# A recurrence feeding routed experts: the inverse grown in PSUM, decays exchanged on TensorE, loads multiplied in place, and a new start

## The chip, the cores and the metric

The kernel runs on one core of one Trainium2 chip. The metric is the device time of one execution in microseconds (us); the time given for a kernel is the median of its runs. The engines are TensorE (PE, with its weight loads as PEld), VectorE (DVE), ScalarE (ACT), GpSimd (POOL) and SyncE (SP, which here only issues DMAs). All numbers are 32-bit floats.

## The reference, cut to what matters

Four batches, eight heads, 768 steps, head size 40. For every step a 40 x 40 state is read by r, decayed by w, changed by a and b, and added to by v and k. The result, 3072 rows of 320, goes through one of eight expert networks (320 to 1024 to 320), chosen for each row by its token number.

```python
for t in range(S):
    y[:, :, t] = einsum('bhd,bhde->bhe', rt, state)
    Sa = einsum('bhde,bhe->bhd', state, at)
    state = state * wt[:, :, None, :] - einsum('bhd,bhe->bhde', Sa, bt)
    state = state + einsum('bhd,bhe->bhde', vt, kt)
x = y.transpose(0, 2, 1, 3).reshape(B * S, H * D)
expert_idx = token_ids * 2654435761 % E
out[expert_idx == e] = maximum(x[expert_idx == e] @ w1[e], 0) @ w2[e]
```

## The kernel before, in words

**Chunks and tiles.** Time is cut into 12 chunks of 64 steps. A tile is one chunk of two batches (two halves of 64 partitions) with all eight heads; there are 24 tiles, u = 0 to 23, and even and odd tiles carry the states of different batches. Inside a chunk, the 64 steps become matrix products: the products of decays up to each step (p) and from each step to the end (q) scale a, b and k, and the dependence of a step on those before it becomes a triangular matrix that has to be inverted, in blocks of 32.

**The plan.** Every step of the attention part is a small function put into a list with a time in ticks (`at_tick`). The list is sorted, and its functions are called in that order. PE, DVE, ACT and POOL carry out their instructions in just this order (`manual_schedule`, L780); SP's DMAs are not in that list before the change, and the framework orders them. Each engine works through its own queue in order and waits where an operand isn't there. One tick is about one tile's work on PE. Tile u is prepared around tick u and goes through the recurrence at tick u + 8 (LAG), so ticks 0 to 7 only prepare, 8 to 23 do both, 24 to 31 only the recurrence.

**Decays** (L216 to L325). Six rounds, each of two chunks, hence four tiles. w is loaded to 128 partitions (four sub-blocks of 32 batch-heads, 32 steps each). DVE clamps it and counts the clamped values into `wbad` (L249, L250), multiplies up p and q in segments of eight steps (L263, L268), and takes products of whole segments (`own`). The two halves of a chunk lie on different partitions, so they exchange their end products through DRAM: store, load, store (L279, L280, L287), and L315 loads the ends again to form `pend` with PE. Then POOL does two wide products (L296, L302) and stores p and q to DRAM as rows (L233), four DMAs each.

**Tile, first part** (`tile_a`). At u - 2, SP loads p, q (L347, L348), a, b, k (L193) to `pl`, `al`, `ql`, `kb`. At u - 1.3, POOL multiplies: `at` = a p (L360), `z` = (b, k) q (L362). PE turns both (t_ps L412, z_ps L379), ACT copies them back. At tick u PE forms a_ps; ACT copies part of it to `pk`, DVE masks the rest to `mk` (L403), POOL makes `no` (L401).

**Inverse** (`group_i`). For four tiles together, DVE builds the inverse of 32 x 32 blocks, one per partition and head, in `ub` in SBUF: POOL fills it with the identity (L428, L429), then 31 times DVE forms `outer` (L444) and adds it to `ub` (L447), spread over 3.4 ticks. Two DVE transposes give `ut` and `ug` (L455, L456). PE uses them in x_ps (at tick u + 7 plus a fraction) and u_ps; ACT and POOL make `xi` and `um`.

**Recurrence** (`tile_s`, `tile_b`). r and v are loaded (L193) and turned on PE one after the other (r_t, v_t). PE's steps are r_ps (r0, r1), c_ps, rc_ps (rc_v, rc_c), nc_ps, s_ps, y_ps, sd_ps. DVE masks rc_ps to `mr` (L581), scales s_ps by `pend` to `sc` (L600), scales y_ps by `py` to `xs` (L618); POOL loads `py` (L510) and stores xs (L621). Within a tick the order is that of STEPS (L200). PSUM is used in three buffers of two banks (`psa`) and two of one bank (`psb`).

**Experts** (L859 on). Once the attention is done, its buffers are given up, SP loads the weights (L86, L88, L799), POOL gathers rows (L805) and scatters results (L836), PE does up_ps and dn_ps. At the end the sum of `wbad` decides whether a slow path has to run. It doesn't with these inputs.

Of the kernel before, what the change touches and what calls it, by code (L numbers as in the profile page):

```python
# [8 lines left out]
F32 = mybir.dt.float32  # L9
# [9 lines left out]
def kernel(  # L19
# [61 lines left out]
    wbad = route.tile([P, 2 * S * B * H // (C * P)], F32)  # L81
# [18 lines left out]
    psa = apool("psa", 3, space=bass.MemoryType.PSUM)  # L100
    psb = apool("psb", 2, space=bass.MemoryType.PSUM)

# [25 lines left out]
    at_r, r1_r = (ring(n, 2, [P, HP, R], gap) for n in ("at", "r1"))  # L128
    r_r = ring("r", 2, [P, HP, P], gaps)
    x_r = ring("x", 3, [P, 2, HP, P], gaps2)  # L130
    z_r = ring("z", LAG + 2, [P, 2, HP, R], gap)


    st_r = ring("st", NG, [R, 2, HP, 2, D], all_of)
    sd_r = ring("sd", NG, [R, 2, HP, 2, D], all_of)
    sc_r = ring("sc", NG, [R, 2, HP, D], all_of)
    at_t_r = ring("at_t", LAG, [P, 2 * HP * C + BLK], lambda t: t[:, 2 * HP * C:])
    en_r = ring("en", 2, [BLK, HP, P], all_of)
# [4 lines left out]
    nc.vector.memset(first[:], 0.0)  # L143
    for be in range(2):
        rows = slice(be * C, (be + 1) * C)
        nc.vector.tensor_tensor(after[rows], upper[rows, rows], ones[rows, rows], op=OP.mult)
        nc.vector.memset(first[be * C:be * C + BLK], 1.0)
        rows = slice(be * C + BLK, (be + 1) * C)
        nc.vector.tensor_copy(xi_r(0)[rows, :, BLK:C], ident[rows, rows].unsqueeze(1).to_broadcast([BLK, H, BLK]))


# [3 lines left out]
    end_dram = [nc.dram_tensor(f"end{i}", (RN, 3, B * H, D), F32) for i in range(NR)]  # L155
# [34 lines left out]
    def load(dst, src, b0, t0, crossed=False):  # L190

        for be in range(2):
            nc.sync.dma_start(dst(be, half(1 - be if crossed else be)),  # L193
                              src[b0 + be, :, t0:t0 + C, :].rearrange("h t e -> t h e"))

    tiles = [dict() for _ in range(NU)]
    plan = []


    STEPS = ["c", "rc_v", "x", "sd", "nc", "rc_c", "u", "a", "r_t", "v_t", "s", "y", "r0", "r1", "at_t", "z"]  # L200

    def at_tick(tick, step=None, order=0):
        if step is not None:
            tick += STEPS.index(step) / len(STEPS)

        def add(f):
            plan.append((round(tick, 4), order, len(plan), f))
            return f
        return add
# [6 lines left out]
    def decays(ri, t0, span, t_ends):  # L216
# [8 lines left out]
        def segs(t):  # L225
            return t[:, 0:HC * D].rearrange("p (s t e) -> p s t e", s=SEG, e=D)


        BH = B * H

        def store(i, src):
            for y in range(2 * RN):
                nc.gpsimd.dma_start(pq_dram[ri][i][y * HC:(y + 1) * HC].rearrange("t bh e -> bh t e"),  # L233
                                    src[y * BH:(y + 1) * BH].rearrange("p (t e) -> p t e", e=D))

        def ends_rows(i):

            return end_dram[ri][:, i:i + 2].rearrange("n x bh e -> n (x bh) e")

        @step  # L240
        def _():
            x["pb"] = pb = work.tile([P, HC * D], F32, tag="pb", name="pb", bufs=1)
            x["qb"] = qb = work.tile([P, (HC + 1) * D], F32, tag="qb", name="qb", bufs=1)
            for y in range(2 * RN):
                src = w.rearrange("b h (n t) e -> (b h) n (t e)", t=HC)[:, ri * 2 * RN + y]
                nc.sync.dma_start(pb[y * BH:(y + 1) * BH], src)
            nc.sync.dma_start(end_dram[ri][:, 2], ones[0:RN * BH, 0:D])
            q = qb[:, 0:HC * D]
            nc.vector.tensor_scalar(q, pb[:], LO, HI, op0=OP.max, op1=OP.min)  # L249
            nc.vector.scalar_tensor_tensor(pb[:], q, 0.0, pb[:], op0=OP.add, op1=OP.not_equal,  # L250
                                           accum_out=wbad[:, ri:ri + 1])

        @step
        def _():
            nc.vector.memset(segs(x["pb"])[:, :, 0, :], 1.0)


        qs = [x_ for x_ in range(SL - 2, -1, -1)]
# [5 lines left out]
        for i in qs:  # L264
            @step
            def _(i=i):
                q = segs(x["qb"])
                nc.vector.tensor_tensor(q[:, :, i], q[:, :, i], q[:, :, i + 1], op=OP.mult)  # L268

        @step  # L270
        def _():

            q = segs(x["qb"])
            x["own"] = own = work.tile([P, SEG, D], F32, tag="own", name="own", bufs=1)
            x["ends"] = ends = work.tile([P, SEG + 1, D], F32, tag="ends", name="ends", bufs=1)
            nc.vector.tensor_copy(own[:, SEG - 1], q[:, SEG - 1, 0])
            for s in range(SEG - 2, -1, -1):
                nc.vector.tensor_tensor(own[:, s], q[:, s, 0], own[:, s + 1], op=OP.mult)
            nc.sync.dma_start(ends_rows(0), own[:, 0])  # L279
            nc.sync.dma_start(ends[:, SEG], ends_rows(1))  # L280

        @step
        def _():
            ends = x["ends"]
            nc.vector.tensor_tensor(ends[:, 0:SEG], x["own"][:],
                                    ends[:, SEG].unsqueeze(1).to_broadcast([P, SEG, D]), op=OP.mult)
            nc.sync.dma_start(ends_rows(0), ends[:, 0])  # L287
            x["rends"] = rends = work.tile([P, SEG, D], F32, tag="rends", name="rends", bufs=1)
            nc.vector.reciprocal(rends[:], ends[:, 0:SEG])
            nc.vector.tensor_scalar(rends[:], rends[:], -1.0, None, op0=OP.mult)  # L290

        @step
        def _():

            p = segs(x["pb"])
            nc.gpsimd.tensor_tensor(p, p, x["rends"][:].unsqueeze(2).to_broadcast([P, SEG, SL, D]), op=OP.mult)  # L296
            store(0, x["pb"][:])

        @step
        def _():  # L300
            q = segs(x["qb"])
            nc.gpsimd.tensor_tensor(q, q, x["ends"][:, 1:].unsqueeze(2).to_broadcast([P, SEG, SL, D]),  # L302
                                    op=OP.mult)
            nc.gpsimd.tensor_copy(x["qb"][:, HC * D:], x["ends"][:, SEG])
            store(1, x["qb"][:, D:])

        for i, f in enumerate(todo):
            at_tick(t0 + span * i / len(todo), order=8)(f)

        @at_tick(t_ends)  # L310
        def _():

            en = en_r(ri)
            for rn in range(RN):
                nc.sync.dma_start(en[rn * B:(rn + 1) * B].rearrange("b hp (two x) -> b (hp two) x", two=2)[:, :, 0:D],  # L315
                                  end_dram[ri][rn, 0].rearrange("(b h) e -> b h e", h=H))

        @at_tick(t_ends + 1.0)
        def _():
            en = en_r(ri)  # L320
            p = bank([P, HP, B * RN], "en_ps")
            for hp in range(HP):
                nc.tensor.transpose(p[0:R, hp, :], en[0:B * RN, hp, 0:R], ident[0:B * RN, 0:B * RN])
            x["pend"] = t = work.tile([P, HP, RN, B], F32, tag="pend", name="pend", bufs=NR)
            nc.scalar.copy(t[0:R].rearrange("p h n b -> p h (n b)"), p[0:R])  # L325
# [4 lines left out]
    def tile_a(u):  # L330
# [5 lines left out]
        @at_tick(u - 2.0)  # L336
        def _():
            x["p"] = pl = work.tile([P, DM], F32, tag="pl", name="pl")
            x["a"] = al = work.tile([P, DM], F32, tag="al", name="al")
            x["q"] = ql = work.tile([P, 2, DM], F32, tag="ql", name="ql")  # L340
            x["kb"] = kb = work.tile([P, 2, DM], F32, tag="kb", name="kb")

            def by_head(t):
                return t.rearrange("t (h e) -> t h e", h=H)
            p_rows, q_rows = (d[rn * C:(rn + 1) * C] for d in pq_dram[ri])
            for be in range(2):
                nc.sync.dma_start(pl[half(be)], of_batches(p_rows, 2 * g + be, 1))  # L347
                nc.sync.dma_start(ql[half(be)], of_batches(q_rows, 2 * g, 2))  # L348
            load(lambda be, rows: by_head(al[rows]), a, 2 * g, n * C)

            load(lambda be, rows: by_head(kb[rows, be]), b, 2 * g, n * C)
            load(lambda be, rows: by_head(kb[rows, be]), k, 2 * g, n * C, crossed=True)

        @at_tick(u - 1.3)
        def _():
            x["at"], x["z"] = at_r(u), z_r(u)

            def view(t):
                return t.rearrange("p (hp two e) -> p hp two e", hp=HP, two=2)
            nc.gpsimd.tensor_tensor(heads(x["at"]), view(x["a"][:]), view(x["p"][:]), op=OP.mult)  # L360
            for be in range(2):
                nc.gpsimd.tensor_tensor(heads(x["z"][:, be]), view(x["kb"][:, be]), view(x["q"][:, be]), op=OP.mult)  # L362
# [639 lines left out]
```

## Time and profile before

| What | us |
|---|---|
| median of the runs | 867.81 |
| lowest and highest of 3 runs | 861.88, 875.35 |
| profiled execution, its own time | 872.0 |
| its span, first to last instruction | 870.1 |
| PE busy in the span | 654.8 |
| DVE busy | 380.2 |
| POOL busy | 317.2 |
| ACT busy | 222.0 |

Busy times overlap, so they don't add up to the span. The page cuts the span into 40 slices of about 21.75 us and gives each engine's busy share in tenths. PE is nearly idle in the first seven, and near full from the tenth on, but for one in the middle where the attention ends and the experts begin. A row of a group reads: line, engine, operation, output and inputs by name, shapes, count. A row of waits reads: engine and line that waited, what released it, total us, times, longest. The clock column is the granted TensorE clock as a share of full speed.

### The profile page before, as it was taken

How to read it: one execution, taken by the hardware profiler on the slowest of the kernel's cores; microseconds unless marked ns; L12 is line 12 of the kernel's file. 1: busy time of each engine (PE TensorE's matmuls, PEld its weight loads, DVE VectorE, ACT ScalarE, POOL GpSimd, SP SyncE). 2: the span in 40 equal slices, each digit the busy share in tenths (PEclk: the TensorE clock that was granted, in tenths of full speed). 3: DMA queues.
4: the chain of work that ended last, by engine and by line, in shares of the span. 5: the costliest groups of instructions: out<-in, count | busy, mean ns of one | idle time of the engine just before them, and what ended most of it. 6: DMA issues, size and time to landing. Idle time of an engine off the chain costs nothing.

```text
span 870.1 us, 27167 instructions
## 1 busy us (share of the span) xinstructions
PE 654.8 (75%) x11952; PEld 501.2 (58%) x11952; DVE 380.2 (44%) x758; ACT 222.0 (26%) x464; POOL 317.2 (36%) x416
## 2 busy tenths in 40 slices
PE   0023532199769986989998999982999999999993
PEld 0012421188658875878787888871556656655652
DVE  7051659567865775666666567121111111011110
ACT  0011211034333442445433434430111111111010
POOL 4617481452274338645534513214022013011101
PEclk9999999998765876678767869996999999999997
DMA  3646484364456446545522223319733226221000
GB/s 70 127 109 137 105 183 96 64 139 86 80 98 140 90 82 120 96 89 110 97 47 41 48 38 60 65 26 303 265 104 100 81 63 200 79 76 36 23 3 25
DMA packets 166793, 82.66 MB, mean 95 GB/s; under 512 B 139982, under 2 KB 156111, under 8 KB 166672
## 3 DMA queue, kind: packets, MB, share of 16 engines
q1 hardware_dynamic: 157264, 56.94, 29.1%
q0 software_dynamic: 9408, 23.95, 11.7%
q8 instruction: 95, 1.56, 0.8%
q14 instruction: 26, 0.21, 0.1%
HBM read 64.78 MB, written 16.40 MB: 93 GB/s over the span
## 4 chain that ended last, share of the span: by engine, by line
PE 60%; DVE 16%; POOL 8%; DMA 7%; issue 4%; SPq 3%; ACT 1%; POOLq 0%; DVEq 0%; ACTq 0%
PE dn_ps L846 12%; PE up_ps L826 11%; PE s_ps L181 6%; PE y_ps L181 5%; PE r_ps L181 4%; DVE ub L447 4%; PE up_ps L822 3%; PE u_ps L181 3%; PE a_ps L181 3%; PE rc_ps L181 3%; PE t_ps L412 3%; DVE outer L444 2%; DMA end<-own 2%; DMA ends<-end 2%; DVE pb L263 2%
## 5 line engine op out<-in xcount | busy, mean ns | idle before, releaser
L846 PE MATMUL dn_ps<-w,ht 128*128 128x320 f32 x384 | 104.9, 433 | 0.0
L447 DVE TENSOR_TENSOR ub<-ub,outer 128x31 f32<-128x31 f32 (+15 forms) x186 | 98.6, 530 | 6.3
L836 POOL DMA_INDIRECT out_dram<-o,idx_all x26 | 25.9, 997 | 187.5 <-ACT o L835 182.6
L826 PE MATMUL up_ps<-xt,w 128*128 128x416 f32 x256 | 93.8, 519 | 0.0
L846 PEld LDWEIGHTS dn_ps<-w,ht 128*128 128x128 f32 x384 | 72.8, 190 | 32.1 <-issue 1.9
L621 POOL DMA_DIRECT2D x_rows<-xs x48 | 27.3, 570 | 159.4 <-DVE outer L444 80.4
L444 DVE TENSOR_TENSOR outer<-ub,nb 128x31 f32<-128x31 f32 (+15 forms) x186 | 72.7, 391 | 21.6 <-POOL ub L429 17.8
L412 PE MATMUL t_ps<-ident,at 64*104 64x64 f32 x192 | 13.0, 269 | 82.2 <-POOL at L360 82.2
L826 PEld LDWEIGHTS up_ps<-xt,w 128*128 128x128 f32 x256 | 47.5, 190 | 45.8 <-issue 45.8
L829 DVE TENSOR_SCALAR ht<-up_ps 128x416 f32<-128x416 f32 x32 | 18.9, 591 | 105.8 <-PE up_ps L826 101.4
L181 PE MATMUL a_ps<-at_t,z_t 40*32 40x64 f32 (+1 forms) x2304 | 52.3, 290 | 13.9 <-ACT z_t L380 7.2
L412 PEld LDWEIGHTS t_ps<-ident,at 64*104 64x104 f32 x192 | 8.9, 157 | 84.0 <-POOL at L360 82.5
L811 DVE COPY xt<-xg_ps 128x384 f32<-128x384 f32 x24 | 12.1, 551 | 102.1 <-PE xg_ps L810 102.1
L181 PEld LDWEIGHTS a_ps<-at_t,z_t 40*32 40x32 f32 (+1 forms) x2304 | 43.0, 157 | 20.8 <-issue 11.0
L181 PE MATMUL x_ps<-ut,no 32*32 32x32 f32 x768 | 19.6, 204 | 45.0 <-DVE ut L455 44.1
L181 PEld LDWEIGHTS s_ps<-x,z 128*64 128x64 f32 (+1 forms) x704 | 36.7, 187 | 19.7 <-issue 19.7
L362 POOL TENSOR_TENSOR z<-kb,ql 128x320 f32<-128x320 f32 x48 | 43.0, 917 | 10.0 <-DMA ql<-q_rows 5.4
L581 DVE TENSOR_TENSOR mr<-rc_ps,after 128x1024 f32<-128x1024 f32 x24 | 29.3, 1221 | 39.5 <-PE rc_ps L181 39.5
L181 PEld LDWEIGHTS x_ps<-ut,no 32*32 32x32 f32 x768 | 16.5, 118 | 47.3 <-DVE ut L455 32.0
L403 DVE TENSOR_TENSOR mk<-a_ps,after 128x512 f32<-128x512 f32 x24 | 16.5, 688 | 56.8 <-ACT pk L399 56.8
L181 PE MATMUL s_ps<-x,z 128*64 128x40 f32 (+1 forms) x704 | 40.0, 280 | 1.0 <-issue 1.0
L296 POOL TENSOR_TENSOR pb<-pb,rends 128x1280 f32<-128x1280 f32 x6 | 17.3, 2888 | 61.2 <-DVE rends L290 61.2
(164 smaller groups left out, 1262.7 us busy)
## 6 DMA issues: line engine op xcount, KB each, us to landing
w<-in_moe_w_dram SPq DMA_DIRECT2D x8, 1280.0 KB
w<-in_moe_w_dram SPq DMA_DIRECT2D x8, 1024.0 KB
ql<-q_rows SPq DMA_DIRECT2D x48, 160.0 KB
pb<-in_w_dram SPq DMA_DIRECT2D x24, 160.0 KB
al<-in_a_dram SPq DMA_DIRECT2D x48, 80.0 KB
kb<-in_b_dram SPq DMA_DIRECT2D x48, 80.0 KB
kb<-in_k_dram SPq DMA_DIRECT2D x48, 80.0 KB
r<-in_r_dram SPq DMA_DIRECT2D x48, 80.0 KB
```

The costliest lines, as they stand in the source:

```text
L181: nc.tensor.matmul(out_, lhsT=lhsT, rhs=rhs, start=start, stop=stop, skip_group_check=True)
L362: nc.gpsimd.tensor_tensor(heads(x["z"][:, be]), view(x["kb"][:, be]), view(x["q"][:, be]), op=OP.mult)
L412: nc.tensor.transpose(p[0:R, be, hp * C:(hp + 1) * C], src[rows, be, hp, 0:R] if crossed else src[rows, hp, 0:R], ident[rows, rows])
L444: nc.vector.tensor_tensor(tv, ub[:, 0:j + 1, j:j + 1].to_broadcast([P, j + 1, m]), nb[:, j, j + 1:].unsqueeze(1).to_broadcast([P, j + 1, m ...
L447: nc.vector.tensor_tensor(o, o, tv, op=OP.add)
L581: nc.vector.tensor_tensor(t[:].rearrange("p two h t -> p (two h) t"), p[:].rearrange("p two (h t) -> p (two h) t", t=C), after[:].unsqueez ...
L621: nc.gpsimd.dma_start(x_rows[r0:r0 + C, :], xs[half(be), :])
L822: nc.tensor.matmul(banks[-1][:], lhsT=w1[rows, w:w + P], rhs=xt[rows, 2, 0:n], start=True, stop=False)
L826: nc.tensor.matmul(p[:], lhsT=w1[:, c * F + f * P:c * F + (f + 1) * P], rhs=xt[:, c, 0:n], start=False, stop=(c == 1))
L829: nc.vector.tensor_scalar(ht[:, f, 0:n], p[:], 0.0, None, op0=OP.max)
L836: st = nc.gpsimd.indirect_dma_start(out=out[:], out_offset=bass.IndirectOffsetOnAxis(ap=idx, axis=0), in_=o[:], in_offset=None, bounds_che ...
L846: nc.tensor.matmul(p[:], lhsT=ht[:, f, j * P:(j + 1) * P], rhs=w2[:, f, :], start=(f == 0), stop=(f == FP - 1))
```

## The change

- **Inverse.** `ub` lies in PSUM (pool `psu`, two banks), filled by ACT. For that, `psa` has two buffers instead of three; sd_ps moves to `psb`. `outer` has one buffer.
- **Decays.** The count into `wbad` leaves. End products of the halves are exchanged by four small PE products with columns of the identity (`ex`); ACT copies them. `pend` comes from one PE transpose. Round 0 runs wholly before tick -7: the wide products are on DVE, and DVE's own 32 x 32 transposes turn p and q on the chip (`lent`, memory of the v tiles), from where the first four tiles load them. Later rounds store p and q from SP instead of POOL. pb and qb have two buffers.
- **Loads in place.** a, b, k are loaded into `at` and `z`, which are multiplied where they lie. The first four tiles load on two queues, SP and ACT, ahead of all, and DVE multiplies them; tile 3's a is loaded at tick 0.2.
- **Order.** SP is in the written order. The memsets of buffers are in the plan, some at tick -9, the rest at -3. x_ps goes to the end of the tick before, z_ps goes ahead of r0. `um`'s first part goes from POOL to ACT. py is loaded 0.7 tick later.
- **r and V** are turned into one psa tile with one ACT copy.
- **Check of w.** After the experts' code, w is loaded again in six pieces and counted on DVE.

```diff
-    psa = apool("psa", 3, space=bass.MemoryType.PSUM)
+    psa = apool("psa", 2, space=bass.MemoryType.PSUM)
     psb = apool("psb", 2, space=bass.MemoryType.PSUM)
+    psu = apool("psu", 1, space=bass.MemoryType.PSUM)
...
-    STEPS = ["c", "rc_v", "x", "sd", "nc", "rc_c", "u", "a", "r_t", "v_t", "s", "y", "r0", "r1", "at_t", "z"]
+    STEPS = ["c", "rc_v", "sd", "nc", "rc_c", "u", "a", "rv", "s", "y", "z", "r0", "at_t", "r1", "x"]
...
+                @at_tick(-9.0 if i < early else -3.0)
+                def _(t=t):
+                    nc.gpsimd.memset(zero(t[:]), 0.0)
...
+        fast = ri == 0
+        wide = nc.vector if fast else nc.gpsimd
...
+            for y in range(2 * RN):
                 src = w.rearrange("b h (n t) e -> (b h) n (t e)", t=HC)[:, ri * 2 * RN + y]
-                nc.sync.dma_start(pb[y * BH:(y + 1) * BH], src)
+                eng = nc.scalar if fast and y % 2 else nc.sync
+                eng.dma_start(pb[y * BH:(y + 1) * BH], src)
-            nc.vector.scalar_tensor_tensor(pb[:], q, 0.0, pb[:], op0=OP.add, op1=OP.not_equal,
-                                           accum_out=wbad[:, ri:ri + 1])
...
+            x["ex"] = ex = bank([P, D], "ex_ps")
+            for y in range(2 * RN):
+                mm(ex[y * BH:(y + 1) * BH], ident[:, (y | 1) * BH:((y | 1) + 1) * BH],
+                   ones[:, 0:D] if y % 2 else own[:, 0])
...
-            nc.sync.dma_start(ends_rows(0), own[:, 0])
-            nc.sync.dma_start(ends[:, SEG], ends_rows(1))
-            nc.sync.dma_start(ends_rows(0), ends[:, 0])
+            nc.scalar.copy(ends[:, SEG], ex)
+            nc.scalar.copy(x["qb"][:, HC * D:], ex)
...
+                wide.tensor_tensor(t, t, by.unsqueeze(2).to_broadcast([P, SEG, SL, D]), op=OP.mult)
+                if fast:
+                    x["pq"[i]] = flat = lent[:, i * BH * D:(i + 1) * BH * D]
+                    nc.vector.transpose(flat.rearrange("p (c e) -> p e c", e=D), src.rearrange("p (t e) -> p e t", e=D))
+                    if i == 0:
+                        nc.gpsimd.dma_start(pq_dram[ri][i][:].rearrange("t bh e -> t (bh e)"), flat)
+                    continue
+                for y in range(2 * RN):
+                    nc.sync.dma_start(pq_dram[ri][i][y * HC:(y + 1) * HC].rearrange("t bh e -> bh t e"),
+                                      src[y * BH:(y + 1) * BH].rearrange("p (t e) -> p t e", e=D))
...
-        @at_tick(u - 2.0)
+        early = u < 2 * NG
+        eng = (nc.sync, nc.scalar)[u % 2] if early else nc.sync
+        held = 3
+        def load_at():
+            x["at"] = at_r(u)
+            load(nc.sync if u == held else eng, x["at"][:], a, 2 * g, n * C)
+        @at_tick(-8.9 + 0.01 * u if early else u - 2.3)
...
+        if u == held:
+            at_tick(0.2)(load_at)
+        @at_tick(-5.0 + u if early else u - 2.7)
...
+            for be in range(2):
+                eng.dma_start(pl[half(be)], rounds[ri]["p"][half(rn), c0 + be * DM:c0 + (be + 1) * DM])
...
+        @at_tick(-4.9 + u if early else u - 1.7)
+        def _():
+            eng = nc.vector if early else nc.gpsimd
+            if u != held:
+                decay_at(eng)
             for be in range(2):
-                nc.gpsimd.tensor_tensor(heads(x["z"][:, be]), view(x["kb"][:, be]), view(x["q"][:, be]), op=OP.mult)
+                z = per_head(x["z"][:, be])
+                eng.tensor_tensor(z, z, view(x["q"][:, be]), op=OP.mult)
...
-            x["u"] = ub = work.tile([P, BLK, BLK], F32, tag="ub", name="ub", bufs=1)
-            nc.gpsimd.memset(ub[:], 0.0)
+            x["u"] = ub = psu.tile([P, BLK, BLK], F32, tag="ub", name="ub")
+            nc.scalar.copy(flat, upper[:, 0:1].to_broadcast([P, BLK * BLK]))
+            nc.scalar.copy(flat[:, ::BLK + 1], ones[:, 0:BLK])
...
-        @at_tick(t0 - 1, "x")
+        @at_tick(t0 - 2, "x")
...
-    for ri in range(NR):
-        decays(ri, max(ri * RN * NG - 6.0, -3.5 + ri), 0.8, max(ri * RN * NG - 2.0, 1.0 + ri))
+    decays(0, -9.0, -8.0, -7.0)
+    decays(1, -8.5, -0.9, 0.6)
+    for ri in range(2, NR):
+        decays(ri, ri * RN * NG - 7.0, ri * RN * NG - 6.0, ri * RN * NG - 4.2)
...
-    with tc.manual_schedule(engines={ET.PE, ET.DVE, ET.Activation, ET.Pool}):
+    with tc.manual_schedule(engines={ET.PE, ET.DVE, ET.Activation, ET.Pool, ET.SP}):
...
+    for i in range(WP):
+        nc.sync.dma_start(wt[:], wq[:, i * m:(i + 1) * m])
+        nc.vector.tensor_scalar(wc[:], wt[:], LO, HI, op0=OP.max, op1=OP.min)
+        nc.vector.scalar_tensor_tensor(wt[:], wc[:], 0.0, wt[:], op0=OP.add, op1=OP.not_equal, accum_out=wbad[:, i:i + 1])
```

## The prediction

> **What bounds the kernel now.** I read the page's busy shares first, then busy time by stretch, then the waits, then the timeline where a wait was long. All durations are of the profiled execution: span 870.1 us, its own time 872.0, which is 4.2 above the median 867.8.
>
> The stretches, cut at the first x_ps product, the first c_ps product (tick 8), the last full tick, the last y and the first up_ps product. Columns: length, then busy time of PE, PEld, DVE, ACT, POOL, granted clock, DMA share, GB/s.
> ```profile
> 0.00:169.30 169.30, 34.83 (x876) 28.93 (x876) 88.84 (x182) 18.35 (x27) 79.56 (x114) 1.00 0.54 111
> 169.30:181.30 12.00, 11.12 (x248) 10.18 (x248) 6.87 (x7) 3.77 (x8) 11.50 (x16) 1.00 0.75 144
> 181.30:390.50 209.20, 180.59 (x4604) 157.20 (x4602) 141.51 (x293) 79.98 (x161) 99.10 (x127) 0.72 0.51 100
> 390.50:495.80 105.30, 97.53 (x2758) 84.42 (x2757) 67.71 (x121) 47.17 (x96) 49.47 (x68) 0.77 0.39 69
> 495.80:588.90 93.10, 84.67 (x2500) 74.61 (x2500) 39.78 (x82) 39.93 (x88) 25.32 (x41) 0.87 0.25 47
> 588.90:608.80 19.90, 3.58 (x12) 1.98 (x12) 3.89 (x12) 1.22 (x5) 10.05 (x12) 0.57 0.99 326
> 608.80:870.10 261.30, 242.46 (x964) 143.85 (x964) 31.55 (x66) 31.58 (x79) 42.22 (x43) 0.97 0.27 88
> ```
> In the first 169 us PE works 35: a start bound by latency. From 181.3 PE is busy 86 to 93%, so TensorE sets the pace; the experts (608.8 on) are TensorE alone. Ten ticks fill 181.3 to 390.5 (20.9 us each), six fill 390.5 to 495.8 (17.55 each), then eight without new A tiles.
>
> What PE and DVE waited for (total, times, longest):
> ```profile
> PE x_ps L181 <- DVE ut L455: 44.1, 4, 31.9
> ...
> DVE ends L285 <- DMA ends<-end: 31.9, 6, 5.7
> ...
> DVE qb L249 <- DMA pb<-in_w_dram: 21.5, 1, 21.5
> ...
> DVE outer L444 <- POOL ub L429: 17.8, 3, 11.5
> ```
> The inverse (ut) is what PE lacks: 31.9 at 169.3, 6.6 at 247.8, 5.4 in the tick from 325.3. The other three rows delay DVE itself.
>
> Three pairs from the timeline (start, length) show why DVE is late:
> ```profile
> 1.84 7.71 DVE L149 COPY xi<-ident 32x256 f32<-32x256 f32 x1
> ...
> 10.35 0.83 DVE L249 TENSOR_SCALAR qb<-pb 128x1280 f32<-128x1280 f32 x1
> ...
> 218.29 3.21 DVE L447 TENSOR_TENSOR ub<-ub,outer 128x220 f32<-128x220 f32 x1
> ...
> 218.53 0.89 POOL L360 TENSOR_TENSOR at<-al,pl 128x320 f32<-128x320 f32 x1
> 219.36 1.69 POOL L362 TENSOR_TENSOR z<-kb,ql 128x320 f32<-128x320 f32 x2
> ...
> 163.88 2.88 POOL L296 TENSOR_TENSOR pb<-pb,rends 128x1280 f32<-128x1280 f32 x1 [25.65 <-DVE rends L290]
> 163.96 2.87 DVE L447 TENSOR_TENSOR ub<-ub,outer 128x60 f32<-128x60 f32 x1
> ```
> A DVE operation with two SBUF inputs lasts as long as the chain of POOL work beside it. DVE operations with a PSUM input do not (durations min/median/max):
> ```profile
> L447 DVE TENSOR_TENSOR ub<-ub,outer x186: 191/387/3241, 118.6 to 536.2; 128x31 f32<-128x31 f32 x12, 128x60 f32<-128x60 f32 x12, 128x87 f32<-128x87 f32 x12, 128x112 f32<-128x112 f32 x12
> L403 DVE TENSOR_TENSOR mk<-a_ps,after x24: 677/690/693, 63.7 to 487.7; 128x512 f32<-128x512 f32 x24
> ```
>
> **The inverse in PSUM.** From the shortest 31-element row (191 ns), an operation is 158 ns + n/0.96. A group is 31 pairs over 5456 elements: 2 x (31 x 0.158 + 5456/960) = 21.2 us, six groups 127. Measured: 98.6 + 72.7 = 171. So 44 us of DVE time are stalls, about 7 per group. With ub in PSUM both operations have at most one SBUF input. [...] No row shows DVE writing PSUM. [...] Filling ub leaves POOL (0.97 + 0.15) for ACT, no row for ACT writing PSUM; 1.0 by z_t (1024 elements in 1.01), hidden, as it is asked for a quarter tick ahead. The 17.8 of POOL waits go.
>
> PSUM has two psa buffers instead of three. Of each tick's six psa tiles PE asks for the next one only after: c, while z is copied (1.01) behind r0, at, r1, x (over 3 us of PE); rv, while mr runs (1.22) behind u and a (2.6 to 4.1); z, while pk and mk run behind rv, s, y; at, behind s, y, z. All covered if DVE is punctual; uncovered see rival three. Turning r and V together makes one 1.01 copy of two 0.59. ACT gets um's upper part (0.37, as um<-u_ps) from POOL's 1.04: ACT stays near 8.4 us per tick of 17.5, hidden.
>
> **The start**, step by step. w: the first 640 KB moved by 4.5 us at the 200 to 236 GB/s of the first slices; DVE began only at 10.35, behind a 7.7 us copy that POOL's memsets held. The copy goes to ACT, so DVE starts at 5. Decays 0: clamp 0.83, memset 0.19, 14 x 0.35, own 1.0, ends 0.33, reciprocal 1.15, 0.24: done at 13.8. The 7.8 us of three DMA trips become four small products and two copies, hidden under seven 0.35 products. The wide products go to DVE (1.49, the row of L250) and each is turned there: 1280 elements at 2.13/1024 is 2.7. p at 18, q at 22.2. Loads of tiles 0 to 3: 22 DMAs x 0.635, split over SP and ACT, issued by 10; they and w take about 13 us at 150 GB/s, landed by 17, hidden. pl, ql out of SBUF: no row; between 2.0 (pl<-p_rows on the chain) and 4: 25.5 for ql. POOL's other memsets stand behind its p store and may hold DVE 18 to 26: at, z of tile 0 (3 x 0.49) end at 27. Then z_ps 1.5, z_t 1.0, a 2.2 and so on: a0 at 32, a1 36.5, a2 41.5. Tile 0's first transpose was at 43.5 before.
>
> DVE then does decays 1 (8.7 and mk): 42; POOL's two products 2.9 each: 47. Their stores moved from POOL (0.79) to SP, where order is now written out: eight at about 0.8 (SP's 512-packet loads are 0.635, POOL's 1024-packet stores 0.79), to 51. Behind them on SP wait w of decays 2 (to 52.8, landed 56.5), pl and ql of tile 4 (which need the stores landed, 56), at and z of tile 4 (60, landed 62). a3 waits for POOL's at3 (48) and ends at 52. DVE: 13 of 18 steps of decays 2 to 62.4, mk, nb 2.1: 66. Up to tick 6.0 come 23 of 31 pairs, 16.6, with 2.8 of decays and 1.4 of mk: 87. There DVE meets decays 3, whose w is late: SP issued tile 5 (66), tile 6 (72), p2 and q2 stores waiting for POOL (80.5), tile 7 (86.3), then w: landed 91. So DVE loses 4; from 91: 8 pairs 4.5, decays 4.3, mk 0.7, ut 2.0, 2 of stalls: 104.5. Then the stretch that took 12.0 before (u, a, z, r): 13 now, since x stands before it. **First c_ps at 117.5 instead of 181.3: -64.** If the SP-to-SBUF trips, stores and w each cost 3 us more, 10 per round: 140, -41; if DVE is not held and w is in time: 105, -76.
>
> **The ticks.** PE's products are the same. The first tick ran cold (20.5); I give it that, and fifteen others 17.5, the mean of the last six of before, where DVE waits were absent: 283 against 314.5, **-31**. x now stands at the end of tick 6 of a group, right behind ut: PE has z, r0, at, r1 (3.4 to 5.2) while DVE has xs, three pairs, ut (0.49 + 1.5 + 1.96 = 3.95), so 0 to 0.6 us of wait per group. SP's 14 loads (0.635, pl and ql 0.55) and a quarter of 12 w and store DMAs come to 11 us per tick. [...]
> ```profile
> 351.90:370.60 18.70, 18.70 (x464) 16.47 (x463) 10.43 (x18) 7.95 (x16) 10.68 (x15) 0.61 0.55 95
> ```
> PE never idle, clock 0.61. [...]
>
> The last eight ticks: c waited 0.62 for ACT's r copy seven times; x or its copy stands between in six: -3.
>
> **w's check** leaves the ticks (1.58 per round, counted above) for the experts: six times 0.83 + 1.49 = 14 us of DVE and 3.9 MB. DVE is busy 31.6 of 261 there. Last in order, it runs under the closing 13 us of dn_ps and ends 0 to 5 late; early, it delays xt by up to 2.4 each: 0 to 14. I take +2.
>
> Sum: 870.1 - 64 - 31 - 3 + 2 = 774 of span; at the same offset to the median (2.3), **772 us**.
>
> **Rivals.**
> One: the start and SP cost more. First c at 145 (-36), ticks 18.5 (-15), check +5: 824 span, 822. For it: SP's in-order waits; against: every item has a row. 0.22.
> Two: the clock stays up more: ticks 16 (-55), start -70: 745. For it: clock 0.87 in the last stretch; against: the row above. 0.12.
> Three: two psa buffers bind. Fully open, the six evictions are 1.01 + 0.59 + 0.59 + 1.22 + 0.69 + 1.01 = 5.1 per tick, in 16 ticks 82, in eight half as much, 22: 774 + 104 = 878, no change. Against: the cover listed. 0.05.
> Four, slower: SP, in written order, becomes the tick's bound: a store waits for POOL, POOL for xs, the loads queued behind for the store. It decides from 24.6 us per tick (774 + 16 x 7.1 = 887, 2% above); at 25 it is 894. SP's own work is 11, so 13 of waits each tick are needed; at and z have 0.6 tick to spare. 0.06.
> My forecast: 0.55.
>
> **Numbers.** Faster by over 2% (about what this measurement can tell from no change): forecast, rivals one and two: 0.89, less 0.02 for unknowns. Same 0.06, slower 0.07. The forecast alone spans 750 to 795; the range takes in rivals one and two: 738 to 830.
>
> **What would show it.** First c_ps between 105 and 130; ut waits of PE under 3 after it; no ub or outer row over 0.7 us; ticks 17 to 18 at clock 0.7 to 0.8; no SP wait ahead of at or z. Wrong if DVE's ub rows lengthen, PE waits for mr, z_t or rv copies, or POOL waits for loads.

## The result, and the profile after

The changed kernel takes 815.44 us (median of four runs, 810.47 to 821.07); the kernel before took 867.75 beside it. The ratio is 0.942 (95% interval 0.933 to 0.952): faster, by 52 us where 96 were forecast. The profiled execution took 821.07 us, span 819.3, so it stands 5.6 above the median; it is the slowest of the four and has the lowest mean clock (0.869 against 0.883 to 0.885). The profiled execution of before stood 4.2 above its median, so the two can be compared.

The same cuts as before, by busy time in each stretch (columns as in the prediction): the start to the first x_ps, to the first c_ps, tick 8, ticks 9 to 17, ticks 18 to 23, the last eight ticks, the change to the experts, the experts. The trace has no record of the clock ahead of 154 us, and that of before none ahead of 199; a 1.00 there is no reading.
```profile
0.00:116.60 116.60, 35.33 (x901) 29.07 (x901) 72.41 (x174) 22.25 (x46) 39.72 (x71) 1.00 0.70 136
116.60:130.20 13.60, 12.36 (x280) 11.14 (x280) 11.55 (x22) 6.76 (x15) 5.45 (x7) 1.00 0.69 132
...
130.23:159.67 29.44, 18.81 (x439) 16.35 (x435) 10.41 (x28) 8.46 (x17) 10.45 (x13) 1.00 0.55 98
159.67:340.20 180.53, 165.35 (x4183) 143.68 (x4177) 111.63 (x257) 80.93 (x160) 67.25 (x88) 0.69 0.55 106
340.20:444.05 103.85, 94.93 (x2754) 82.16 (x2749) 54.70 (x116) 52.11 (x98) 37.24 (x53) 0.80 0.39 74
...
444.05:531.80 87.75, 81.74 (x2473) 72.66 (x2468) 39.86 (x84) 43.33 (x88) 19.10 (x36) 0.88 0.28 52
531.80:550.80 19.00, 3.52 (x12) 1.98 (x12) 3.48 (x11) 1.22 (x5) 8.43 (x10) 0.53 0.99 333
550.80:819.30 268.50, 248.09 (x964) 146.02 (x964) 45.17 (x85) 31.47 (x79) 45.96 (x45) 0.96 0.31 101
```
Term by term, from the two profiled executions (the last eight ticks end with the last y, at 531.2, 0.6 ahead of the cut in the rows):

| Term of the sum | Predicted | Measured |
|---|---|---|
| start, to the first c_ps (181.3 before) | -64 | 130.2: -51.1 |
| ticks 8 to 23 (314.4 before) | -31 | 313.8: -0.6 |
| last eight ticks | -3 | -5.8 |
| change to the experts | 0 | -0.5 |
| experts and end, w's check | +2 | +7.2 |

The inverse did what was worked out for it. Its two rows by tile (durations min/median/max, first and last start), and who waited:
```profile
L484 DVE TENSOR_TENSOR outer<-ub,nb x186: 175/357/425, 78.4 to 477.3; 128x31 f32<-128x31 f32 x12, 128x60 f32<-128x60 f32 x12, 128x87 f32<-128x87 f32 x12, 128x112 f32<-128x112 f32 x12
L487 DVE TENSOR_TENSOR ub<-ub,outer x186: 198/366/432, 78.6 to 477.5; 128x31 f32<-128x31 f32 x12, 128x60 f32<-128x60 f32 x12, 128x87 f32<-128x87 f32 x12, 128x112 f32<-128x112 f32 x12
...
  PE x_ps L216: 4.4, 4
```
The longest row fell from 3241 ns to 432, the sum of both rows is 127.5 us (62.5 and 65.0) where 127 were forecast, and PE's wait for ut fell from 44.1 us to 4.4 (not through PSUM, as the fourth experiment shows). The time was lost to other waits (total, times, longest):
```profile
PE ex_ps L216 <- DVE own L283: 44.7, 6, 12.5
...
DVE qb L268 <- DMA pb<-in_w_dram: 24.3, 3, 13.2
...
ACT z_t L423 <- DMA pl<-x_all: 17.3, 1, 17.3
DVE eid L713 <- DMA tok<-in_moe_token_ids_dram: 15.1, 1, 15.1
...
PE t_ps L453 <- DVE mr L624: 10.6, 1, 10.6
```
The first three belong to the start. The last two are one new wait in tick 8: the token numbers' load stands at tick 8 in SP's written order, lands late, DVE waits for it with mr behind it, and PE waits for mr. The third loss, in ticks 9 to 17, is in no row of waits. PE was idle there for 15.2 of 180.5 us, before for 28.6 of 188.7: the waits did go, but PE's own busy time for the same products grew from 160.1 to 165.4, at a mean clock of 0.69 before and after. PE now ran at half clock for 40.8 us and for 34.1 us on end, before for 20.5 at most:
```profile
195.20:236.00 40.80, 38.91 (x843) 34.07 (x837) 26.39 (x54) 16.83 (x35) 12.01 (x12) 0.50 0.46 85
283.90:318.00 34.10, 33.27 (x685) 29.08 (x683) 15.73 (x37) 13.30 (x28) 14.39 (x14) 0.50 0.56 84
```

### The profile page after: what moved, and what is told of

Its sections match the earlier page's. It is cut to its first block, busy times and chain, and to the rows that moved or that the text cites. A ratio compares the mean times of both kernels' runs of the same rounds, so it can differ in the third digit from the quotient of the medians.

```text
span 819.3 us, 27116 instructions
## 1 busy us (share of the span) xinstructions
PE 660.2 (81%) x11982; PEld 503.1 (61%) x11982; DVE 349.2 (43%) x772; ACT 246.5 (30%) x508; POOL 233.6 (29%) x318
## 4 chain that ended last, share of the span: by engine, by line
PE 66%; issue 8%; DVE 8%; DMA 6%; SPq 5%; POOL 3%; ACT 1%; ACTq 0%; POOLq 0%; DVEq 0%
PE dn_ps L891 11%; PE up_ps L871 9%; PE s_ps L216 7%; PE y_ps L216 6%; PE r_ps L216 4%; PE a_ps L216 4%; PE u_ps L216 4%; PE rc_ps L216 3%; PE t_ps L453 3%; PE up_ps L867 3%; PE x_ps L216 2%; PE sd_ps L216 2%; PE c_ps L216 2%; DMA xg<-x_rows,src_all 2%; PE nc_ps L613 2%
## 5 line engine op out<-in xcount | busy, mean ns | idle before, releaser
L487 DVE TENSOR_TENSOR ub<-ub,outer 128x31 f32<-128x31 f32 (+15 forms) x186 | 65.0, 349 | 6.4
L484 DVE TENSOR_TENSOR outer<-ub,nb 128x31 f32<-128x31 f32 (+15 forms) x186 | 62.5, 336 | 3.2
L216 PEld LDWEIGHTS s_ps<-x_all,z 128*64 128x64 f32 (+1 forms) x704 | 36.6, 187 | 18.1 <-issue 18.1
L422 PE MATMUL z_ps<-ident,z 64*104 64x64 f32 x384 | 29.5, 265 | 19.9 <-DVE z L399 14.2
L423 ACT COPY z_t<-z_ps 104x1024 f32<-104x1024 f32 x24 | 24.3, 1012 | 56.2 <-PE z_ps L422 38.9
L880 ACT COPY o<-dn_ps 128x320 f32<-128x320 f32 x24 | 10.2, 425 | 101.6 <-PE dn_ps L891 101.6
L216 PE MATMUL s_ps<-x_all,z 128*64 128x40 f32 (+1 forms) x704 | 39.6, 280 | 0.0
L399 POOL TENSOR_TENSOR z<-z,ql 128x320 f32<-128x320 f32 x40 | 34.6, 872 | 16.4 <-DMA z<-in_k_dram 13.5
L422 PEld LDWEIGHTS z_ps<-ident,z 64*104 64x104 f32 x384 | 25.1, 160 | 22.4 <-DVE z L399 14.5
L867 PE MATMUL up_ps<-xt,w 64*128 64x416 f32 x128 | 30.6, 580 | 8.3 <-DVE xt L856 3.2
```

What stands on the lines that cost most here:

```text
L216: nc.tensor.matmul(out_, lhsT=lhsT, rhs=rhs, start=start, stop=stop, skip_group_check=True)
L399: eng.tensor_tensor(z, z, view(x["q"][:, be]), op=OP.mult)
L422: nc.tensor.transpose(p[0:R, i, c0:c0 + C], x["z"][half(i), be, hp, 0:R], ident[half(i), half(i)])
L484: nc.vector.tensor_tensor(tv, ub[:, 0:j + 1, j:j + 1].to_broadcast([P, j + 1, m]), nb[:, j, j + 1:].unsqueeze(1).to_broadcast([P, j + 1, m ...
L487: nc.vector.tensor_tensor(o, o, tv, op=OP.add)
L867: nc.tensor.matmul(banks[-1][:], lhsT=w1[rows, w:w + P], rhs=xt[rows, 2, 0:n], start=True, stop=False)
```

## The experiments

Two theories for the ticks. One: a few named waits in SP's order and DVE's order took the gain. Two: the clock took it, and falls by something other than PE's idle time. For the start: the gain is one large part, or several, less what new waits in order cost. Each ratio below is to the kernel before on the same chip.

### Token numbers loaded early

```diff
+    @at_tick(-8.6)
+    def _():
+        nc.sync.dma_start(tok[:], tok_h.bitcast(I32).rearrange("(p c two) -> p c two", p=P, two=2))
     def routing():
-        nc.sync.dma_start(tok[:], tok_h.bitcast(I32).rearrange("(p c two) -> p c two", p=P, two=2))
```


> The changed kernel with the load of the token numbers moved from tick 8 to the very start; nothing else. Theory A (the written order of SP costs what the ticks were to gain): the wait of DVE for the token numbers (15 us, which holds mr and so PE for 10.6 us in tick 8) goes, first c_ps stays near 130, tick 8 falls from 29.4 to about 19 to 20.5, and the time by 9 to 11 us. Theory B (TensorE's granted clock sets the ticks): the wait goes, but the ticks behind it slide against the clock's windows, and ticks 8 to 23 together may give back any part of it: time lower by 0 to 10, and ticks 9 to 23 differ from the 284 us of the changed kernel although nothing in them was edited.

Measured: 799.13 us, ratio 0.933 (0.923 to 0.942). Tick 8 fell from 29.4 to 19.5: the wait was that load. But ticks 9 to 17, which the edit doesn't touch, fell by 10 as well:
```profile
149.30:319.86 170.56, 150.68 (x4182) 129.75 (x4176) 109.68 (x257) 80.69 (x160) 67.36 (x86) 0.77 0.57 110
```
The same products, idle time no shorter (19.9 us), busy time 14.7 us shorter, clock 0.77 instead of 0.69. The time fell by 16 us, more than either theory had; that ticks changed which nothing had edited is theory B's sign.

### w's check one piece per expert

```diff
     for e in range(E):
+        wt = mwork.tile([P, m], F32, tag="wt", name="wt")
+        if 1 <= e <= WP:
+            nc.sync.dma_start(wt[:], wq[:, (e - 1) * m:e * m])
...
+        if 1 <= e <= WP:
+            check(e - 1, wt)
```


> The changed kernel with the six pieces of the check of w done one per expert (1 to 6), on DVE between the expert's last ht and the next expert's xt, instead of all in expert 1. If the check is what lengthened the experts (expert 1 took 36.6 us, the others 29.7; 605 to 612 at half clock), expert 1 falls to 30 and the time by 6 to 7 us. Rival: the re-load of w (3.9 MB) is what delays the experts' weights: then the time stays.

Measured: 810.11, ratio 0.942 (0.933 to 0.952); experts 248.7 instead of 255.3. Behind it, DVE's timeline of the changed kernel in expert 1 (start, length):
```profile
588.17 0.59 DVE L874 TENSOR_SCALAR ht<-up_ps 128x416 f32<-128x416 f32 x1
590.13 0.83 DVE L932 TENSOR_SCALAR wc<-wt 128x1280 f32<-128x1280 f32 x1 [1.37 <-DMA wt<-in_w_dram]
...
592.41 0.59 DVE L874 TENSOR_SCALAR ht<-up_ps 128x416 f32<-128x416 f32 x1
593.32 0.83 DVE L932 TENSOR_SCALAR wc<-wt 128x1280 f32<-128x1280 f32 x1 [0.33 <-DMA wt<-in_w_dram]
```
The framework put all six pieces there, so ht, which PE needs, stands behind pieces that themselves wait for w. Spread out, the check costs nearly nothing: experts and end together take 261.8, before the change 261.3. The total doesn't show it: the ratio is that of the changed kernel. (The half clock in expert 1, which the expectation puts at 605 to 612, is at 594.5 to 601.3 in the trace; 605 to 612 is at full clock.)

### Decays of round 1 early

```diff
-    decays(1, -8.5, -0.9, 0.6)
+    decays(1, -8.5, -6.9, -2.5)
```


> The changed kernel with round 1 of the decays spread over ticks -6.9 to -2.5 instead of -0.9 to 0.6, so that DVE does half of it while it waits for q of tile 0, and PE's four ex_ps products no longer stand between z and a of tile 0 waiting for DVE until 41.7. Theory A: PE's queue was the missed wait; a of tile 0 starts at 36 to 38 instead of 42, the stores of round 1 at 40 to 43 instead of 50.7, first x_ps at 105 to 109 instead of 116.6, time lower by 8 to 11 us. Rival: the start is set by SP's chain of loads behind w of round 3, which gains only what SP gains at the stores: 4 to 6 us. By theory B the ticks may give a part back either way.

Measured: 802.20; first c_ps at 122.5 instead of 130.2. Its executions lie between 794.7 at a mean clock of 0.889 and 816.0 at 0.868, too far apart for a ratio. DVE's longest wait for w fell from 13.2 to 7.4 us, and it began on w of round 2 at 56.95 instead of 64.80: 7.8 earlier, as the first c_ps is. The first a_ps came at 40.1, only 1.9 earlier (36 to 38 were expected): until 36.0 PE stood before another product of round 1, which turns its end products for `pend`.

### The inverse back in SBUF

```diff
-            x["qb"] = work.tile([P, (HC + 1) * D], F32, tag="qb", name="qb")
+            x["qb"] = work.tile([P, (HC + 1) * D], F32, tag="qb", name="qb", bufs=1)
-            x["u"] = ub = psu.tile([P, BLK, BLK], F32, tag="ub", name="ub")
+            x["u"] = ub = work.tile([P, BLK, BLK], F32, tag="ub", name="ub", bufs=1)
```


> The changed kernel with ub back in SBUF (filled by ACT as now, psa still two buffers; qb in one buffer to make room, which nothing waits for). If PSUM's freedom from POOL is worth what the sum gave it, ub and outer rows reach 2 to 3 us again, DVE loses some 20 to 40 us in all, PE waits for ut again (5 us and more per group), and ticks 8 to 23 grow by 10 to 20 us; first x_ps later by 2 to 6. Theory B: DVE has time to spare in the ticks and the clock sets their length: ticks 8 to 23 within 8 us of the 314 of the changed kernel, time within 10.

Measured: 824.03, ratio 0.957 (0.948 to 0.967). First c_ps 3.9 later; ticks 8 to 23 take 313.8, as with PSUM, though DVE is busy 13 us more in ticks 9 to 17 (124.7 to 111.6) and its longest rows are at 3.0 and 3.2 us again. PE waits 4.5 us for ut, against 4.4: theory B. The intervals of the two ratios overlap. A third `psa` buffer was not tried.

(qb goes to one buffer, so that ub fits.)

### The exchange back through DRAM, and the turn back through DRAM

```diff
-            for y in range(2 * RN):
-                mm(ex[y * BH:(y + 1) * BH], ident[:, (y | 1) * BH:((y | 1) + 1) * BH],
-                   ones[:, 0:D] if y % 2 else own[:, 0])
+            nc.sync.dma_start(ends_rows(0), own[:, 0])
+            nc.sync.dma_start(ends[:, SEG], ends_rows(1))
```


> One part undone: in all six rounds of decays the halves exchange their end products through DRAM again (store, load), not with four products on TensorE. Theory A, the exchange on TensorE is a small part of the start's gain, and in round 1 it costs, since its four products stand ahead of a of tile 0: round 0 loses two trips of 2.6 us less the 2.5 us of products that hide them, +3; round 1 no longer holds TensorE, -8: first c_ps at 122 to 130, time within 6 us of the changed kernel. Theory B, the exchange is what brought the start forward: first c_ps at 140 or later, time 825 or more.

Measured: 827.38, ratio 0.966 (0.953 to 0.979); first c_ps at 142.2, 12.0 later. My theory A is refuted: the exchange is a real part. DVE's waits in the first 125 us:
```profile
DVE ends L305 <- DMA ends<-end: 15.2, 3, 8.5
```
Round 0 ends 8.4 us later (z of tile 0 is multiplied at 37.1, not 28.7), yet the first a_ps starts at 42.7, not 42.0. So for a_ps the changed kernel had thrown those 8 us away again, as PE's timeline there shows:
```profile
30.56 0.70 PE L453 MATMUL t_ps<-ident,at 64*104 64x64 f32 x5
41.74 0.24 PE L216 MATMUL ex_ps<-own,ident 128*32 128x40 f32 x1 [10.48 <-DVE own L283]
...
42.04 1.18 PE L216 MATMUL a_ps<-at_t,z_t 40*32 40x64 f32 x64
```
and, from 31.38 on, ACT's:
```profile
31.38 1.39 ACTq L383 DMA_DIRECT2D ql<-x_all  x2
32.80 1.01 ACT L423 COPY z_t<-z_ps 104x1024 f32<-104x1024 f32 x1 [17.34 <-DMA pl<-x_all]
33.71 0.59 ACT L412 COPY at_t<-t_ps 104x512 f32<-104x512 f32 x1
```
PE has turned tile 0 at 31.3. ACT copies it late, behind the issue of tile 3's loads, by 34.3. From there a_ps could start, but PE stands until 41.7 before the ex_ps products of round 1, which come ahead of it in the written order. With the exchange undone nothing stands there, and 34.3 + 8.4 is 42.7, as measured.

```diff
-                if fast:
+                if False:
...
-            if not early:
+            if True:
```


> One part undone: round 0 stores p and q to DRAM by four DMAs each and tiles 0 to 3 load them from there, instead of DVE turning them on the chip. Theory A, the turn on the chip gains a few us only: eight stores at 0.73 to 1.2 us and a trip of some 4 us against two transposes of 2.7 us: first a_ps 3 to 6 us later, first c_ps at 132 to 136, time 818 to 822. Theory B, the turn is what brought the start forward: first c_ps at 145 or later, time 830 or more.

Measured: 827.96, ratio 0.968 (0.955 to 0.981); first a_ps 6.1 later, first c_ps 5.8 later, as theory A said. The median is 6 over its range, the profiled execution (820.9) within it.

### The three mends together

The first three edits in one kernel.

> The three edits together: the token numbers loaded at tick -8.6, the check of w as one piece per expert, the decays of round 1 at ticks -6.9 to -2.5. Theory A, the three delays are independent and lie one behind the other on the path: first c_ps at 122 (130.2 less 7.7), tick 8 near 20 instead of 29.4, experts near 249 instead of 255: 25 us less than the changed kernel, 790, at a granted clock of 0.68 in ticks 9 to 17; if the clock there is up as it was with the early token numbers alone (0.75), 780. Theory B, the clock gives back what the waits leave: half-clock stretches grow, ticks 8 to 23 stay near 314 and the time stays over 800.

Measured: 802.81, ratio 0.936 (0.923 to 0.948). First c_ps 121.8, tick 8 18.5, experts 248.8: all three mends held, 26 us. But the total is no better than with the token numbers alone: the clock in ticks 9 to 17 was 0.68, and they took 179.7 instead of 170.6. By the total this is theory B, though ticks 8 to 23 took 305.1, not 314.

### Extra products on TensorE

A product that nothing reads, ahead of s, in 22 ticks; then the same on `ident[0:32, 0:32]` and `ones[0:32]`.

```diff
             def _():
+                mm(bank([P, 512], "fill"), ident[:], ones[:].unsqueeze(1).to_broadcast([P, 4, P]))
                 p = bank([P, 2, HP * D], "s_ps")
```


> The changed kernel with one extra product per tick, 128 x 128 by 512 columns, ahead of s, whose result nothing reads. Theory A, the granted clock follows how much of the array works in a stretch (it falls behind stretches of s, y, z and r, which use few columns): with the full product in there the clock of ticks 9 to 17 rises from 0.68 to 0.8 or more, half-clock stretches of over 30 us vanish, and these ticks take 19 or less each in spite of the extra 0.45 to 0.9 us: 800 or less. Theory B, the clock doesn't see this: every one of 16 ticks is longer by 0.5 to 0.9, time 823 to 830.

> The control to the run with the full filler: the extra product has the same 512 columns but uses 32 x 32 of the array, so it lasts as long (2.1 us in two passes) and fills little of it. Theory A, the clock follows how much of the array works: the clock of ticks 9 to 17 stays at 0.65 to 0.76, where all kernels without a full filler lie (the full filler gave 0.81), and these ticks take 185 to 200. Theory B, any product of this length moves the ticks against the clock's windows, or the one run was luck: clock 0.8 or more, ticks 9 to 17 near 174.

Measured: full filler 837.50, ratio 0.977 (0.965 to 0.989); 32 x 32 filler 863.74, ratio 0.998 (0.993 to 1.003). The fillers by tile, full and then small (ns min/median/max):
```profile
L216 PE MATMUL fill<-ones,ident x44: 592/1061/1220, 151.0 to 527.4; 128*128 128x512 f32 x44
```
```profile
L216 PE MATMUL fill<-ones,ident x44: 584/1056/1057, 149.9 to 560.1; 32*32 32x512 f32 x44
```
and ticks 9 to 17 with the one and the other:
```profile
159.94:333.88 173.94, 153.42 (x4200) 124.67 (x4195) 109.89 (x255) 80.38 (x160) 66.70 (x87) 0.82 0.56 107
```
```profile
160.48:357.81 197.33, 183.99 (x4200) 147.25 (x4195) 111.39 (x257) 81.04 (x160) 67.29 (x88) 0.65 0.51 98
```
Same place, same median length, same count of products: 23 us apart in nine ticks, at clocks of 0.82 and 0.65. The profiled execution of the small one, 869.35, is 5.6 above its median, but all executions agree: their mean clocks over the span are 0.888 to 0.896 in the four with the full filler, 0.835 to 0.865 in the ten with the small one. In this pair the clock followed how much of the array worked: 0.82 with 128 x 128 of it, 0.65 with 32 x 32. Rows and columns changed together, so the pair doesn't say which of them counts. That these ticks were shorter with the full filler than in the changed kernel (180.5) would alone show nothing: kernels without a filler took 167.0 to 182.7 there. The filler cost 2.1 us a tick where 0.45 to 0.9 were expected, and as a mend it fails: the total is 22 us above that of the changed kernel.

With the three mends I then tried shorter full fillers in ticks 8 to 23.

> The three edits (early token numbers, spread check, early round 1) and a full 128 x 128 filler of 128 columns ahead of s in ticks 8 to 23. It costs 2.1 x 128/512 = 0.5 us a tick, 8.4 in all. Theory A, a short full product is enough to hold the clock: ticks 9 to 17 at 0.8, 9 x (17.3 + 0.5) = 160 against 180 for the three alone, total near 785. Theory B, it is too short to count: clock 0.65 to 0.76, ticks as without it plus 0.5 each, total 800 to 812.

> As the run with 128 columns, with 256: 1.05 us a tick, 16.8 in all. Theory A, the clock needs some length of full work: if 128 columns do too little and 512 enough, this lies between, clock 0.75 to 0.82, total 790 to 800. Theory B, the filler does nothing to the clock: total 808 to 820.

Measured: 802.67 (ratio 0.931, 0.923 to 0.938) and 807.20 (0.932, 0.923 to 0.941); clock 0.69 in ticks 9 to 17 of both, so neither raised it. That is theory B, and the second total is 0.8 under its range.

### w of rounds 2 and 3 loaded early

```diff
-        decays(ri, ri * RN * NG - 7.0, ri * RN * NG - 6.0, ri * RN * NG - 4.2)
+        decays(ri, {2: -3.5, 3: 1.2}.get(ri, ri * RN * NG - 7.0), ri * RN * NG - 6.0, ri * RN * NG - 4.2)
```


> The three edits, and w of rounds 2 and 3 of the decays loaded at ticks -3.5 and 1.2 instead of 1.0 and 5.0, so that in SP's written order it stands ahead of the stores of p and q of the round before. With the three alone DVE waited 18.5 us for w, of which some 13 after the first load of all, and the first c_ps came at 121.8. Theory A, DVE's waits for w set the end of the first inverse: they go, first c_ps at 109 to 113, time 790 to 796 at the same clock (0.67 in ticks 9 to 17). Theory B, what DVE then does earlier waits for something else (a of tile 3, a buffer of pb that is still being stored): first c_ps at 117 or later, time within 4 us of the three alone (803).

Measured: 788.87 (six runs), ratio 0.918 (0.912 to 0.924), the fastest. First c_ps at 117.1, 4.7 earlier than with the three mends; clock 0.69 in ticks 9 to 17. DVE's waits in the first 121.8 us, with the three mends and then with this:
```profile
DVE qb L268 <- DMA pb<-in_w_dram: 18.5, 3, 7.5
```
```profile
DVE mk L446 <- ACT pk L442: 7.5, 3, 4.4
DVE pb L275 <- DMA ql<-q_rows: 6.8, 1, 6.8
DVE qb L268 <- DMA pb<-in_w_dram: 4.9, 1, 4.9
```
Of 13.6 us of waiting for w, 6.8 came back as a wait at the products of decays, with a load of q as its last releaser. DVE began on w of rounds 2 and 3 at 49.6 and 85.4, where with the early round 1 alone it was 57.0 and 97.8. So the truth lies between the theories: for c_ps, B was right by its bound; for the time, neither range held, and some of the gain came from other ticks.

## Why the prediction was right or wrong

**The start, -64: direction and place right, 13 us too much.** What failed is the size of two terms, the time of SP's stores ("to 51") and, behind them, that of w: "landed 56.5" for round 2 and "landed 91" for round 3. DVE began on them 8.3 and 14.5 us later:
```profile
64.80 0.83 DVE L268 TENSOR_SCALAR qb<-pb 128x1280 f32<-128x1280 f32 x1 [13.23 <-DMA pb<-in_w_dram]
...
105.52 0.83 DVE L268 TENSOR_SCALAR qb<-pb 128x1280 f32<-128x1280 f32 x1 [6.16 <-DMA pb<-in_w_dram]
```
With that, "DVE loses 4" became 19.4. From w of round 3 on the sum held: 24.7 us to the first c_ps, 26.5 forecast. Ahead of it, DVE had done round 1 of the decays at 47.6, not 42, as it waited 8.3 us for p and q of the first tiles from the chip's own copy; and SP's eight stores of round 1, ahead of w, ran from 50.7 to 58.4:
```profile
50.66 2.94 SPq L321 DMA_DIRECT2D p_rows<-pb  x4
53.76 4.67 SPq L321 DMA_DIRECT2D q_rows<-qb  x4
58.47 2.44 SPq L264 DMA_DIRECT2D pb<-in_w_dram  x4
```
Two experiments show that this is the path: with round 1 early, w of round 2 and the first c_ps both came 7.8 earlier; with the loads of w early too, the first c_ps came at 117.1. I had written 117.5; as the loads of w stand elsewhere there than in my sum, that the two numbers meet is partly luck.

"Four small products and two copies, hidden" failed too, but cost little here. In round 0 they were hidden, and undoing the exchange cost 12.0 at the first c_ps. In round 1 they stood on PE ahead of a_ps: the first a_ps came at 42.0, not at 32 or earlier; 7.7 of it by this, 2.0 by loads of tile 3 that ACT issued ahead of its copies (z_ps was done at 30.8, z_t began at 32.8). But DVE waited only 1.3 us for what came of that a_ps (mk, at 44.97), and then stood for w in any case.

Where the 51 come from: undone one at a time, the exchange is worth 12.0, the turn on chip 5.8, the inverse in PSUM 3.9. The other 29 were not undone one by one. Most of the 51 lies between the first a_ps and the first x_ps (115.6 us before, 74.6 after): there DVE's busy time fell from 64.3 to 46.1, and its waits for late a tiles from 20.0 to 6.2, for the ends' exchange from 16.2 to 0, for POOL's fill of ub from 11.5 to 0, while that for w rose from 0 to 19.4. How the new order of loads and the check's leaving share in this stays open.

**The ticks, -31: wrong, -0.6.** Two terms. The first tick, "I give it that" (20.5), was 29.4: I counted SP's moved DMAs for loads and stores, and missed the token numbers' load, which SP's written order moved too. The larger is "fifteen others 17.5". I took the mean of ticks in which DVE's waits were absent, and with it their clock of 0.77. Ticks 18 to 23 did take 17.3, but ticks 9 to 17, which ran at 0.69 before, ran at 0.69 again with half of PE's idle time gone, and took 20.1. The waits that went did not move the clock.

What does? The clock's records lie on a grid of 3.41 us. For 1174 of its windows, in 14 traces (from each one's first record to 440 us), I summed over the matmul records columns x (rows x columns of the weights)/16384, each record spread over its time, so a product on the full array counts fully, one on 32 x 32 a sixteenth:
```
sum in a window   windows   the next one at full clock
under 900           344       0%
900 to 1050         116      17%
1050 to 1150        180      47%
1150 to 1250        111      65%
1250 to 1350        118      92%
over 1350           305     100%
```
One cut at 1122 tells the next window's clock in 88% of cases; PE's busy share does so in 69% at its best cut, "as it was" in 70%. A window at full clock gets more done and so has a larger sum (in the changed kernel about 1340 on average, at half clock about 970), but that isn't all: among the 574 windows at half clock, a cut at 1186 is right in 87%, where "half again" is in 70%. Rows alone, without the columns of the weights, do nearly as well as both (87% of all), so which of them counts stays open. Three windows of the changed kernel, PE busy in all of each:
```profile
225.87:229.28 3.41, 3.41 (x124) 3.18 (x124) 3.31 (x7) 0.67 (x2) 1.84 (x3) 0.50 1.00 164
...
232.70:236.11 3.41, 3.41 (x67) 3.41 (x66) 1.22 (x4) 0.91 (x2) 0.00 (x0) 0.50 0.62 108
236.11:239.52 3.41, 3.41 (x84) 3.01 (x81) 2.78 (x7) 1.85 (x4) 2.15 (x4) 1.00 0.81 195
```
The first holds a and u, on at most 40 x 64 of the array: sum 653, and half clock stays. The second holds s and y: sum 1341, and full clock follows. (In the expectation of the full filler I had it the other way round, with the clock falling behind s and y.) How an edit to tick 8 moves the clock of ticks 9 to 17 is then open to one reading, which no run tested: if the windows don't move with the kernel (counted from the first instruction, their grid lies at 1.24 us before and at 0.60 in the changed kernel), the same products fall differently into them, and dense work that a window's edge cuts in two may reach the cut in neither. The pair of fillers supports the cause; the cut is read from traces, and why 256 columns didn't suffice is not settled, nor why ticks 18 to 23 had the higher clock (0.80 to 0.69 in the changed kernel) in all these traces but that of the full filler.

I had gone by the row of 0.61, in which PE is never idle for 18.7 us: that was right, as the clock stood low there without idle time. I then took one clock for all ticks, which was not right.

**The last eight ticks, -3:** -5.8, at a clock of 0.88, before 0.87; the sign is as forecast, the size nearly double. PE's wait of c for ACT's r copy, on which it rested, fell from 4.9 us to 0.5.

**w's check, +2:** +7.2. I saw the early case ("early, it delays xt") but weighed it too little; it was ht behind w's own loads.

**The inverse: right.** 127 us forecast, 127.5 measured, and PE's waits for ut after the first c_ps were 2.9, under the 3 named. The 0.96 elements a ns in it is the slope of rows of before: 31 elements in 191 ns, 1280 in 1492 (L250); and mk's row, 512 elements from PSUM in 690 ns, is 157 + 512/0.96, nearly the same fixed part as from SBUF. But no gain from it shows beside PE: back in SBUF, ticks 8 to 23 took the same 313.8, and PE's wait for ut was the same.

**Rivals.** One (822) is the nearest in time, but with a later first c_ps (145) than the 130.2 measured and shorter ticks (18.5) than the mean 19.0 of ticks 9 to 23; its sum also leaves out the -3 of the last eight ticks, with which its span is 821. The measured 815 lies outside what the forecast alone spanned (750 to 795), and inside the range only because that takes in rival one, whose terms err in opposite directions: partly luck. Two is refuted: ticks 9 to 17 took 20.1, not 16, with PE idle for 15.2 us in all. Three is refuted: its 5.1 us of evictions per tick would be 46 in these nine ticks alone. Four, too: no tick is bound by SP but the first.

## What to carry to other kernels

When order is written out by hand, list every instruction that this newly puts in line, also those outside the part you change: one small load cost 10 us here, and four tiny products held the first a_ps for 8. Follow the loads behind what you add to a queue: w behind eight stores set the end of the start. Before you count a removed wait as gain on TensorE, ask at what clock the freed time runs: here, in windows of 3.41 us, how much of the array worked told the next window's clock in 88% of cases, TensorE's busy share in 69%. Undo the parts one at a time: of 51 us at the start, the inverse, whose longest DVE row fell from 3.2 us to 0.4, was worth 4.

## What the hardware showed that I had not expected

- Two kernels that differ by one product's shape (128 x 128 or 32 x 32 of the array, both of a median 1.06 us a pass) differ by 0.82 to 0.65 in the granted clock of ticks 9 to 17.
- DMAs that ACT had to issue held the copies behind them: z_ps was done at 30.8, z_t began 2.0 us later, as tile 3's loads were issued (30.05 to 32.77).
- With ub in PSUM, DVE's two rows of the inverse cost what they would in SBUF without stalls: 158 ns + n/0.96, from a row with SBUF alone before (191 ns for 31 elements), gives 127 us for both, and 127.5 were measured (62.5 reading PSUM, 65.0 reading and writing it).
